# Loading order at the start of a fused SSM and SwiGLU kernel: tile 3 moved to ScalarE's queue behind a wait, up weights moved forward

## The chip, the cores and the metric

One core of one Trainium2 chip. The metric is device time in microseconds (us).

## The reference, cut to what matters

A layer norm over 2048 tokens of 448 features feeds a state-space model `s` and a gated feed-forward network; the output is `x + s * silu(ffn)`.

```python
xn = _layernorm(x, axis=-1)                      # x: 2048 x 448, bf16
s = _A_ref(xn, ...)                              # complex diagonal scan, D = P = 448
g = _silu((_silu(xn @ w_gate) * (xn @ w_up)) @ w_down)   # 448 -> 1792 -> 448
return x + s * g
```

The tokens are cut into 16 tiles of 128 rows. The first quarter is tiles 0 to 3. The 448 features are three blocks of 128 and a fourth block of the last 128, which overlaps the third.

## The kernel before: the parts that matter

The start loads tile 0 and the first weights on SyncE, tiles 1 and 2 on ScalarE:

```python
warm(11, D)                                     # filler matmuls until tile 0 is there
load_x1(0)                                      # SyncE
load_x(1, 3, nc.scalar)                         # ScalarE: tiles 1 and 2
nc.scalar.activation(of_table[:], half_pi[:], ACT.Sqrt)    # brings the table in
load_w(Wg, B_w_gate, 0, 512)                    # 384 KB (3 blocks), then 128 KB (last block)
load_x1(3)
load_w(Wu, B_w_up, 0, 512, part=0)              # 384 KB
for h in (H2, H1):                              # last block in two halves of 64 rows
    nc.sync.dma_start(out=Wu[h, KF, 0:512], in_=B_w_up[blk(KF), 0:512][h])
load_gu(512, 1024)                              # and so on: more weights, tiles 4 to 7, ...
```

The layer norm of tiles 0 to 3, in the order of the program (VectorE works in order; tile 2's sums are done by ScalarE):

```python
ln_stats(0); ln_std(0); act_part(2, 0)          # VectorE, ScalarE, ScalarE
ln_stats(1, ...); ln_std(1)
...                                             # tiles 0 and 1: norm, transposes, copies
act_part(2, 1)                                  # ScalarE: squares of tile 2
nc.scalar.activation(std[:, 2:3], ..., ACT.Sqrt, ...)
ln_stats(3)                                     # VectorE: statistics of tile 3
ln_std(3)
for n in range(2, TQ):                          # TQ = 4
    ln_inverse(n)                               # VectorE
    ln_norm(n)                                  # VectorE: xn[2], then xn[3]
```

On TensorE the first blocks run as a left half (tiles 0 and 1: gate, then up) and a right half (tiles 2 and 3). The transposes of tiles 2 and 3 sit among the up matmuls of the left half, in program order. Each transfer is also tied to a slot: from the ninth on, a SyncE load waits until an earlier one with its slot has landed.

## Time and profile before

| | before |
|---|---|
| median of the first 3 runs | 181.67 us (181.45 to 182.03) |
| span of the profile | 180.0 us |
| TensorE busy | 175.6 us, 98% |
| tile 0 lands | 3.1 us |
| tile 3 issued, lands | 2.17, 6.37 us |
| first matmul of the right half | 9.47 us |

The span is counted from the first instruction. A landing is the start of the issue plus the profile's time from issue to landing. The lines behind this table stand in the prediction. From the right half on TensorE has no gap, so that moment fixes the end.

### The profile page before, as it was taken

The numbers are of one execution on the slowest core, as the hardware profiler recorded it, in microseconds if no ns is written. First come the engines' busy times: TensorE is split into PE (matmuls) and PEld (weight loads), VectorE is DVE, ScalarE is ACT, GpSimd is POOL, SyncE is SP. The second block draws the span as 40 slices with busy tenths as digits, with TensorE's granted clock in tenths as the row PEclk, the third lists the DMA queues.
The fourth block names the chain that finished last, engine by engine and source line by source line (L and its number), as shares of the span: only waits on it lengthen the run. The fifth ranks groups of instructions, "written<-read, shape, count | busy, mean of one in ns | idle before, by whom it ended". The sixth has DMA issues, their size and how long they took to land.

```text
span 180.0 us, 3870 instructions
## 1 busy us (share of the span) xinstructions
PE 175.6 (98%) x1505; PEld 91.4 (51%) x1505; DVE 164.8 (92%) x271; ACT 122.1 (68%) x258; POOL 14.8 (8%) x24
## 2 busy tenths in 40 slices
PE   8999999999999999999999999999999999999992
PEld 3685555555555555555454444444444555555551
DVE  4869799999999989989999999999999999998872
ACT  4858779997779999299589997789676223101110
POOL 7022400000000000701400000000000000000001
PEclk9999999999999999999999999999999999999998
DMA  6996466889000000044000250000000001001111
GB/s 182 321 361 181 101 131 78 167 240 374 13 0 4 2 0 4 0 85 136 2 4 0 47 69 5 0 4 0 0 4 0 0 26 55 27 0 51 51 55 51
DMA packets 25074, 12.72 MB, mean 71 GB/s; under 512 B 14944, under 2 KB 25056, under 8 KB 25056
## 3 DMA queue, kind: packets, MB, share of 16 engines
q1 hardware_dynamic: 24512, 12.18, 26.1%
q10 hardware_dynamic: 416, 0.30, 0.5%
q8 instruction: 12, 0.20, 0.4%
q14 instruction: 6, 0.05, 0.1%
q0 software_dynamic: 128, 0.00, 0.0%
HBM read 7.23 MB, written 1.84 MB: 50 GB/s over the span
## 4 chain that ended last, share of the span: by engine, by line
PE 95%; DVE 2%; DMA 1%; issue 0%
PE gp L482 25%; PE hd L631 24%; PE up L482 20%; PE y L669 12%; PE pb L482 12%; PE one L482 2%; DMA x_all<-in_A_x_dram 1%; DVE stats_of L269 1%; DVE xn L283 0%; DVE ob L695 0%; DVE t L691 0%; DVE mv L272 0%; PE tp L335 0%; DVE rstd L708 0%; PE y L675 0%
## 5 line engine op out<-in xcount | busy, mean ns | idle before, releaser
L482 PE MATMUL gp<-xT,Wg 64*128 64x512 bf16 (+2 forms) x400 | 82.4, 364 | 0.0
L482 PE MATMUL up<-xT,Wu 64*128 64x512 bf16 (+2 forms) x400 | 82.2, 364 | 0.0
L482 PEld LDWEIGHTS <-Wg 64*128 64x128 bf16 x444 | 38.4, 94 | 22.5
L482 PEld LDWEIGHTS <-Wu 64*128 64x128 bf16 x428 | 38.2, 94 | 17.7 <-DMA Wu<-in_B_w_up_dram 0.2
L631 PE MATMUL hd<-Wd,Vt 128*128 128x448 bf16 x224 | 43.5, 352 | 0.0
L618 ACT ACTIVATE gs<-gp 128x512 bf16<-128x512 f32 x52 | 32.1, 617 | 10.7 <-PE gp L482 10.7
L619 ACT ACTIVATE us<-up 128x512 bf16<-128x512 f32 x52 | 32.4, 623 | 0.0
L631 PEld LDWEIGHTS <-Vt 128*128 128x128 bf16 x224 | 21.8, 98 | 20.5 <-DVE H_im L556 0.2
L636 ACT ACTIVATE sg<-hd 128x448 bf16<-128x448 f32 x16 | 8.4, 536 | 29.7 <-PE hd L631 29.6
L482 PE MATMUL pb<-xT,BT 64*128 64x512 bf16 (+1 forms) x224 | 21.9, 349 | 0.0
L623 DVE TENSOR_TENSOR Vt<-gs,us 128x2048 bf16<-128x2048 bf16 (+1 forms) x16 | 17.2, 1073 | 0.1
L482 PEld LDWEIGHTS <-BT 64*128 64x128 bf16 x224 | 11.7, 94 | 10.4 <-issue 0.4
L562 DVE TENSOR_TENSOR_SCAN bu_re<-rcol,H_re,ere 128x512 bf16<-128x512 f32 x12 | 15.2, 1270 | 0.1
L517 ACT ACTIVATE bu_re<-pb 128x512 bf16<-128x512 f32 (+1 forms) x20 | 10.0, 530 | 4.2 <-PE pb L482 4.1
L562 DVE TENSOR_TENSOR_SCAN bu_im<-rcol,H_im,eim 128x512 bf16<-128x512 f32 x9 | 11.4, 1262 | 0.0
L669 PE MATMUL y<-C,H_re 128*128 128x448 bf16 x48 | 11.0, 353 | 0.0
L319 ACT ACTIVATE xn<-x_all,off_of,rstd 128x384 bf16<-128x384 bf16 (+1 forms) x16 | 8.3, 622 | 3.4 <-POOL off_of L313 3.4
L691 DVE TENSOR_TENSOR t<-t,sg 128x448 f32<-128x448 f32 x15 | 9.4, 625 | 1.1
L527 ACT ACTIVATE bu_im<-bu_re 64x512 bf16<-64x512 bf16 x16 | 10.0, 628 | 0.3
L695 DVE TENSOR_TENSOR sg<-t,x_all 128x448 bf16<-128x448 f32 x15 | 9.4, 625 | 0.5
L556 DVE TENSOR_TENSOR tmp<-bu_im,ST 128x2048 bf16<-128x2048 bf16 x8 | 9.7, 1216 | 0.0
L669 PE MATMUL y<-C,H_im 128*128 128x448 bf16 x36 | 8.8, 352 | 0.0
(126 smaller groups left out, 191.0 us busy)
## 6 DMA issues: line engine op xcount, KB each, us to landing
out_dram<-sg SPq DMA_DIRECT2D x15, 112.0 KB, 1.7
Wd<-in_B_w_down_dram SPq DMA_DIRECT2D x1, 1568.0 KB, 10.1
Wg<-in_B_w_gate_dram SPq DMA_DIRECT2D x3, 384.0 KB, 4.9
Wu<-in_B_w_up_dram SPq DMA_DIRECT2D x3, 384.0 KB, 5.3
x_all<-in_A_x_dram SPq DMA_DIRECT2D x1, 896.0 KB, 5.2
x_all<-in_A_x_dram SPq DMA_DIRECT2D x2, 224.0 KB, 5.9
Wg<-in_B_w_gate_dram SPq DMA_DIRECT2D x3, 128.0 KB, 4.7
Wu<-in_B_w_up_dram SPq DMA_DIRECT2D x2, 128.0 KB, 5.3
```

Of the source, the lines that this page charges most:

```text
L482: mm = nc.tensor.matmul(out[:, a:b], lhsT=w[h, d, :], rhs=xT[h, d, q * W + c0 + a : q * W + c0 + b], start=(first and m == 0 and cut is cu ...
L517: nc.scalar.activation(to, pair[i][0], ACT.Copy)
L527: nc.scalar.activation(out[a], in_[b], ACT.Copy)
L556: nc.vector.tensor_tensor(out=of(out, n), in0=of(a, n), in1=of(b, n), op=op)
L562: nc.vector.tensor_tensor_scan(out=T["b"][c][:, k, :], data0=rcol[:, k : k + 1].to_broadcast([P, W]), data1=T["e"][c][:, k, :], initial=in ...
L618: nc.scalar.activation(gs[:, i + j, :], gp_[:], ACT.Silu)
L619: nc.scalar.activation(us[:, i + j, :], up_[:], ACT.Copy)
L623: nc.vector.tensor_tensor(out=Vt[:, f0 : f0 + n, :], in0=gs[:, 0:n, :], in1=us[:, 0:n, :], op=ALU.mult)
L631: nc.tensor.matmul(hd, lhsT=Vt_of[q][:, fi, j * P : (j + 1) * P], rhs=Wd[:, fi, :], start=(fi == 0), stop=(fi == NF - 1),)
L669: nc.tensor.matmul(y[:, c0:c1], lhsT=h, rhs=C2[:, n, c0:c1], start=(n == 0), stop=(n == NS - 1))
L691: nc.vector.tensor_tensor(out=t[:], in0=y, in1=sg[:, c0:c1], op=ALU.mult)
L695: adds.tensor_tensor(out=ob, in0=t[:], in1=x_all[:, m, c0:c1], op=ALU.add)
```

## The change

Its evident intent: free SyncE of one issue, so that the up weights come third on its queue; keep tile 3 from disturbing tile 0 by the wait; load the last up rows to all 128 partitions at once; split the large down load.

```diff
-    load_x1(0)
+    first = load_x(0, 1)
     load_x(1, 3, nc.scalar)
     of_table = ctile([P, 1], F32, "of_table")
     nc.scalar.activation(of_table[:], half_pi[:], ACT.Sqrt)
+    behind(nc.scalar, first)
+    load_x(3, 4, nc.scalar)
     load_w(Wg, B_w_gate, 0, 512)
-    load_x1(3)
-    load_w(Wu, B_w_up, 0, 512, part=0)
-    for h in (H2, H1):
-        nc.sync.dma_start(out=Wu[h, KF, 0:512], in_=B_w_up[blk(KF), 0:512][h])
+    load_w(Wu, B_w_up, 0, 512)
     load_gu(512, 1024)
...
-        nc.sync.dma_start(out=Wd[:], in_=B_w_down.rearrange("(ft p) d -> p ft d", p=P))
+        for half in (slice(0, NF // 2), slice(NF // 2, NF)):
+            nc.sync.dma_start(
+                out=Wd[:, half, :], in_=B_w_down.rearrange("(ft p) d -> p ft d", p=P)[:, half, :]
+            )
```

(The helper `load_x1` goes, and `load_x` returns its instruction. `behind` is an empty instruction that waits for a transfer.)

More of the change, by code (lines that the diff above doesn't have):

```diff
@@ L134 @@
     SYNC = mybir.DependencyInfo(mybir.DependencyClass.Sync, mybir.DependencyReason.DATA)
-    def load_x1(n):
-        nc.sync.dma_start(out=x_all[:, n, :], in_=x2d[n * P : (n + 1) * P, :])
     def load_x(n0, n1, eng=nc.sync):
-        eng.dma_start(
+        return eng.dma_start(
             out=x_all[:, n0:n1, :],
```

## The prediction

> **What bounds the kernel now.** I read the page first (busy shares and the forty slices), then the chain of waits, then the busy time by stretch, then the timeline of the first ten microseconds with each early transfer's time to landing. The page says where to look:
>
> ```profile
> span 180.0 us, 3870 instructions
> PE 175.6 (98%) x1505; PEld 91.4 (51%) x1505; DVE 164.8 (92%) x271; ACT 122.1 (68%) x258; POOL 14.8 (8%) x24
> PE   8999999999999999999999999999999999999992
> DMA  6996466889000000044000250000000001001111
> PE 95%; DVE 2%; DMA 1%; issue 0%
> ```
>
> TensorE is busy 98% of the span, and 95% of the chain that ended last is its matmuls. The transfers are dense only in the first ten slices and short bursts later. So a change to loads can act in one way only: by moving the moment at which TensorE is fully fed. The busy times by stretch (columns: stretch, length, PE, PEld, DVE, ACT, POOL, granted clock, DMA share, GB/s) say where that moment is:
>
> ```profile
> 0.00:5.90 5.90, 4.93 (x44) 2.14 (x45) 3.35 (x23) 2.80 (x7) 3.73 (x14) 1.00 0.73 222
> 5.90:10.00 4.10, 4.10 (x112) 3.65 (x110) 3.02 (x12) 3.66 (x10) 0.00 (x0) 1.00 1.01 322
> 10.00:177.00 167.00, 166.60 (x1360) 85.61 (x1354) 158.00 (x236) 115.60 (x242) 10.84 (x10) 1.00 0.24 60
> 177.00:180.00 3.00, 0.00 (x0) 0.00 (x0) 0.40 (x1) 0.00 (x0) 0.22 (x1) 0.82 0.13 38
> ```
>
> From 10 us to the end of the matmuls TensorE is busy 166.60 of 167.00; the missing 0.40 is its own end at 176.6. A load that lands earlier there gains nothing. Before 5.9 us TensorE runs filler matmuls and waits for tile 0 through the layer norm. What the change can touch is between 5.9 and 10 us, where the columns say busy but the ends of matmuls are modelled, so I look at the instructions:
>
> ```profile
> 0.72 2.37 DMA x_all<-in_A_x_dram
> 3.12 0.64 DVE stats_of L269
> 5.91 1.83 PE L482 MATMUL one<-xT,Wg 64*128 64x128 bf16 x44
> 6.35 0.63 DVE L269 BATCH_NORM_STATS2 stats_of<-x_all 128x6 f32<-128x448 bf16 x1
> 7.54 0.24 PEld L482 LDWEIGHTS <-Wu 64*128 64x128 bf16 x5
> 7.96 0.33 PEld L482 LDWEIGHTS <-Wu 64*128 64x128 bf16 x7 [0.18 <-DMA Wu<-in_B_w_up_dram]
> 8.20 0.31 PEld L335 LDWEIGHTS <-xn 64*128 64x128 bf16 x6
> 9.47 0.22 PE L482 MATMUL gp<-xT,Wg 64*128 64x128 bf16 x1
> ```
>
> The reader is to see three things. Tile 0 lands at 3.1 us and starts everything. The only wait of TensorE for a weight in the whole run is 0.18 us at 7.96, for the last up rows. The tile-3 statistics start at 6.35, just when tile 3 lands.
>
> The early landings, from issue start plus the time to landing of each issue (in us): tile 0 0.72+2.4=3.1; tiles 1 and 2 (ScalarE) 0.73+2.9=3.6; gate 384 KB 1.18+4.0=5.2; gate 128 KB 1.65+4.2=5.85; tile 3 2.17+4.2=6.35; up 384 KB 2.64+4.9=7.55; the two up halves of 64 rows 3.12+4.8=7.9 and 3.72+4.4=8.1.
>
> **What the Trainium skill says.** (1) "DMA: Bandwidth & Descriptors", section "Queues, rings and completion order": SyncE and ScalarE each own a ring on each of the same 16 DMA engines, and an engine takes turns between rings, packet by packet. The trace agrees: the 224 KB of tiles 1 and 2 landed at 3.6 on ScalarE's ring while 384 KB of gate, issued 0.45 us later on SyncE's, took until 5.2. (2) Same page, "Issuing engines are not separate DMA queues": a second issuing engine only saves sequencer time. An issue on SyncE is seen to take 0.4 to 0.6 us. (3) "SBUF — State Buffer", section "Door 1: The DMA port swizzle": a transfer to partitions 0 to 63 reaches only half of the ports. The trace fits: between 6.25 and 7.25 us, when the two 64-row halves should pass, the engines moved 212 GB/s, against 361 in the microsecond before and 351 in the one after. (4) "TensorE: Matmul & The Clock Gate", section "Wait — 56ns, not 53.3ns?": matmuls follow each other at columns over 2.4 GHz plus 2.5 ns when warm. The trace agrees: the 512-column matmuls of one array half start at 32.99, 33.20, 33.42, 33.63 us, 0.21 to 0.22 apart.
>
> **The change part by part.**
>
> Tile 3 to ScalarE behind tile 0. Removed from SyncE: one issue of 0.43 us and 112 KB ahead of the up weights. Added on ScalarE: a wait for tile 0 (about 3.1 us) and an issue of about 0.46 us (as its first one took), so 3.15 to 3.6. ScalarE is idle from 2.7 to 4.01 in the timeline, waiting for tile 0's mean: free. First data comes about 1 us after an issue (the engines start moving about 1.75 us, the first issue is at 0.72), so tile 3 shares the engines from about 4.15 and, by analogy with tiles 1 and 2, lands 2.4 to 2.9 us after issue: 5.6 to 6.1 instead of 6.35. VectorE reaches its statistics only after the copies that end at 6.28. Gain at most 0.07 us; and the next thing, the inverse deviation of tile 2 at 7.34, waits for ScalarE's square root that ends at 7.30, not for tile 3. So tile 3 earlier is worth nothing on TensorE's path.
>
> Up weights third, last 128 rows in one load. The issues move from 2.64, 3.12, 3.72 to about 2.17 and 2.65. But the stream is limited by rate: 0.98 MB lie ahead of the up weights in both kernels, since tile 3 only changes ring. The 384 KB should land at 7.2 to 7.55. Its last rows follow at the full rate: 128 KB at 360 GB/s is 0.36 us, against about 0.7 us for two half-rate loads. So all of the up weights are in by about 7.6 to 7.9 instead of 8.1, while what TensorE first asks for, the upper half, came at 7.9 before. Most of the 0.18 us wait may go. Ceiling: TensorE's work between 5.91 and 9.47 is 16 steps of 0.056 and 6 of 0.109 on gate (1.54), 14 of 0.109 on up (1.53), two tiles' transposes at about 0.13 each and the parameters' 0.06: 3.39 of 3.56 us. So no order of loads can win more than about 0.17 us there. And part is not free: the transposes of tile 2 started at 8.20 after a normalisation that ended at 8.02, so TensorE can come forward about 0.1 us before it waits for that instead. My estimate: 0.1 us.
>
> Ring slots. The order listing shows that each SyncE transfer, from the ninth in the program, waits for the one eight earlier. There is one transfer fewer up front, so the next gate load goes at about 3.1 rather than 4.36; the last 128 up rows of the second group now wait for tile 3 (about 6.0) and go about when they went before (6.00). Later loads come some 0.4 us earlier (the half-rate loss). Nobody on the path wants them: the second weight group landed at 9.3 to 11.1 and is used from about 12.4; tiles 4 and 5 (VectorE waited 1.22 us for them until 12.62) come earlier, which helps VectorE, not TensorE. Worth 0.
>
> Down weights in two loads. One more issue of about 0.57 us on SyncE at about 37 us; the load landed at 36.6+10.1=46.7 and its first reader starts at 59.5. Even 1 us later costs 0.
>
> Sum: 0.1 us gained, 181.67 to about 181.57.
>
> **The rivals.** (a) The new transfer on ScalarE's ring takes turns with the gate weights, which were ahead of it in one ring before. Gate's last 128 KB landed at 5.85 and is first needed at about 6.08 (the fourth matmul pair after 5.91): slack 0.2 us. Tile 3's 0.115 MB at 360 GB/s could push it back by up to 0.32 us: a new wait of 0.1 us on gate, which would eat the gain: 181.7. For it: the same round robin that made tiles 1 and 2 fast. Against it: at 4.15 only some 0.19 MB of gate is left. (b) Tile 3 lands late (after 6.28) because it is issued 1 us later. VectorE is in order, so its statistics would hold back tile 2's normalisation too, with some 0.1 us of slack: 0.5 us late would be 0.4 us on the end: 182.0. Against it: its ring is empty. (c) The freed ring slots and the full-rate load give more than I count, all of the 0.17 us and an earlier normalisation: 181.4. (d) Everything is hidden and only the scatter shows: 181.67 give or take 0.3.
>
> **Range and chances.** The scatter of the kernel before is 181.45 to 182.03. Around 181.55, with the rivals from 181.4 to 182.0 and a median's scatter of about 0.2, I take 181.1 to 182.1. A gain of 2% is 3.6 us, twenty times the ceiling of 0.17; a loss of 2% would need a stall that no margin above is near to. Faster 0.01, within 2% 0.98, slower 0.01.
>
> **What would show it.** Right: up weights' wait near 7.96 gone or under 0.1 us; the matmuls that start at 9.47 start at 9.3 to 9.45; the rate does not dip at 6.25 to 7.25; TensorE busy from there to 176.5; the down loads land before 50. Wrong: a wait of TensorE for gate weights near 6.1 (rival a); tile-3 statistics starting after 6.5 (rival b); any wait of TensorE for a weight or a tile after 12 us; an end of the matmuls that moves by more than 0.3 us.

## The result, and the profile after

The changed kernel takes 183.06 us in the median of 6 runs (182.59 to 183.66), against 181.7 (181.45 to 182.03) for the kernel before in the same rounds: ratio 1.0076, 95% interval 1.0056 to 1.0096. That is within 2%, as forecast, but 1.4 us slower and outside the range 181.1 to 182.1.

The page of the changed kernel: span, busy times, TensorE in forty slices.

```profile
span 181.3 us, 3871 instructions
PE 175.5 (97%) x1505; PEld 91.5 (50%) x1505; DVE 164.7 (91%) x271; ACT 122.1 (67%) x258; POOL 14.6 (8%) x24
PE   8789999999999999999999999999999999999992
```

No engine has more work than before (TensorE 175.5 against 175.6). The 1.3 us by which the span grew are idle time, and the slices place it in the second and third (7 and 8 where it was 9 and 9). The busy times by stretch (the columns are those of the prediction: stretch, length, PE, PEld, DVE, ACT, POOL, clock, DMA share, GB/s):

```profile
0.00:5.90 5.90, 4.61 (x44) 2.18 (x44) 3.36 (x23) 2.80 (x7) 3.74 (x14) 1.00 0.70 207
5.90:10.00 4.10, 2.99 (x79) 2.44 (x72) 1.99 (x8) 2.30 (x6) 0.00 (x0) 1.00 1.09 355
...
10.70:177.80 167.10, 167.10 (x1375) 86.19 (x1370) 158.00 (x237) 116.26 (x245) 10.22 (x9) 1.00 0.23 58
```

From 5.9 to 10 us TensorE is busy 2.99 us where it was busy all 4.10. From the first matmul of the right half on it is busy 167.10 of 167.10 us; the same piece of work in the kernel before:

```profile
9.47:176.50 167.03, 167.03 (x1375) 86.14 (x1370) 157.83 (x237) 116.13 (x244) 10.39 (x9) 1.00 0.24 61
```

The same 1375 matmuls in the same time: everything behind the right half's start is merely moved. The question is what held that start back. The chain of waits of the changed kernel, its first 11 us (start, length, what):

```profile
0.73 2.44 DMA x_all<-in_A_x_dram
...
3.24 4.85 DMA x_all<-in_A_x_dram
...
8.11 0.64 DVE stats_of L265
...
9.12 0.41 DVE xn L279
```

Before, the chain ran through tile 0, TensorE's first matmuls and nothing more of DMA. Now it runs through tile 0, then straight into a second transfer of 4.85 us, tile 3, and from there over VectorE. The instructions in the timeline:

```profile
3.24 0.36 ACTq L138 DMA_DIRECT2D x_all<-in_A_x_dram  x1
...
7.54 0.64 PEld L478 LDWEIGHTS <-Wu 64*128 64x128 bf16 x12
...
8.11 0.63 DVE L265 BATCH_NORM_STATS2 stats_of<-x_all 128x6 f32<-128x448 bf16 x1 [1.76 <-DMA x_all<-in_A_x_dram]
...
9.57 0.17 PEld L331 LDWEIGHTS <-xn 64*128 64x128 bf16 x8 [1.39 <-DVE xn L279]
...
10.70 0.22 PE L478 MATMUL up<-xT,Wu 64*128 64x128 bf16 x1
```

Read it beside the lines of before in the prediction, and beside this one, tile 2's normalisation before:

```profile
7.62 0.40 DVE L283 TENSOR_SCALAR xn<-x_all,mv,rstd 128x448 bf16<-128x448 bf16 x1
```

The up weights load without a wait at 7.54: the wait of 0.18 us is gone. But tile 3's statistics start at 8.11 instead of 6.35, so tile 2 is normalised at 9.12 instead of 7.62, TensorE's transposes of tile 2 start at 9.57 instead of 8.20, the right half at 10.70 instead of 9.47, and the last matmul group at 177.51 instead of 176.19. Tile 3 landed at 3.24 + 4.8 = 8.04 us, 1.67 later than before.

### The profile page after: what moved, and what is told of

Same layout as the page of the kernel before. It is cut to its first block, busy times and chain, and to the rows that moved or that the text cites. A ratio compares the mean times of both kernels' runs of the same rounds, so it can differ in the third digit from the quotient of the medians.

```text
span 181.3 us, 3871 instructions
## 1 busy us (share of the span) xinstructions
PE 175.5 (97%) x1505; PEld 91.5 (50%) x1505; DVE 164.7 (91%) x271; ACT 122.1 (67%) x258; POOL 14.6 (8%) x24
## 4 chain that ended last, share of the span: by engine, by line
PE 93%; DMA 4%; DVE 1%; issue 0%; DVEq 0%; ACTq 0%
PE gp L478 25%; PE hd L627 23%; PE up L478 20%; PE y L665 12%; PE pb L478 12%; DMA x_all<-in_A_x_dram 4%; PE one L478 0%; DVE stats_of L265 0%; DVE xn L279 0%; DVE ob L691 0%; DVE t L687 0%; PE gp L331 0%; DVE mv L268 0%; PE y L671 0%; PE up L331 0%
```

## The experiments

The theory to test: tile 3's late landing is the whole loss, and it lands late because a transfer is served behind all that were issued before it, on either queue. The wait delays its issue until SyncE has the up weights issued ahead of it. Rivals: the up or down loads or the shifted slots cost; ScalarE's queue, or its wait, is slow in itself; VectorE's order is the greater part.

| kernel | tile 3's queue | issued | KB issued ahead | landed | right half starts | median us | ratio (95%) |
|---|---|---|---|---|---|---|---|
| before | SyncE | 2.17 | 848 | 6.4 | 9.47 | 181.7 | 1 |
| changed | ScalarE, wait | 3.24 | 1744 | 8.0 | 10.70 | 183.06 | 1.0076 (1.0056 to 1.0096) |
| t3_sync | SyncE | 2.17 | 848 | 6.3 | 9.41 | 181.63 | 0.9992 (0.9978 to 1.0005) |
| t3_alone | ScalarE, wait | 2.88 | 1296 | 8.3 | 10.91 | 182.83 | 1.0061 (1.0045 to 1.0078) |
| t3_sync_late | SyncE | 3.18 | 1360 | 7.9 | 10.51 | 182.93 | 1.0061 (1.0045 to 1.0078) |
| up_gated | ScalarE, wait | 3.08 | 848 | 5.9 | 10.37 | 182.17 | 1.002 (0.9995 to 1.0044) |
| t3_at_once | ScalarE | 1.2 | 720 | 6.2 | 9.67 | 181.91 | 1.0001 (0.9982 to 1.002) |
| t3_no_wait | ScalarE | 1.29 | 720 | 5.5 | 10.23 | 182.28 | 1.0027 (1.0001 to 1.0054) |
| t3_mid | SyncE | 2.65 | 1232 | 7.75 | 10.31 | 182.66 | 1.0033 (1.0012 to 1.0054) |
| dve_order | ScalarE, wait | 2.99 | 1360 | 8.4 | 10.71 | 183.09 | 1.0067 (1.0049 to 1.0085) |
| up_one_load | SyncE | 2.17 | 848 | 5.8 | 9.48 | 181.76 | 0.9995 (0.998 to 1.0009) |

The KB are those of the loads (tiles and weights) whose issue began earlier; the 1744 of the changed kernel include 384 KB of gate issued only 0.06 us before. "Right half" is the start of its first matmul in the profile. The 181.7 us of before are from the rounds of the changed kernel; in the rounds of the other rows before had medians of 181.82, 181.82 and 181.69, and each ratio is taken to those of its own rounds. The landings are of one profile each. They fall into two groups, 5.5 to 6.4 us with 720 to 848 KB ahead and 7.75 to 8.4 with 1232 to 1744; within a group the KB do not order them.

**t3_sync: tile 3 back, the rest of the change kept.**

```diff
-    behind(nc.scalar, first)
-    load_x(3, 4, nc.scalar)
     load_w(Wg, B_w_gate, 0, 512)
+    load_x(3, 4)
     load_w(Wu, B_w_up, 0, 512)
```

> The changed kernel with tile 3 put back on SyncE between the gate and the up weights, no wait on ScalarE; up rows in one load and down weights in two stay. Theory (the tile's late landing is the whole loss, because a transfer is served behind all that were issued before it on either queue): tile 3 lands at 6.2 to 6.4 us, its statistics start near 6.3, no wait for a weight near 8 us, 181.4 to 181.8 us. Rival (the loss comes from the up or down loads or from the shifted ring slots): stays near 183.

As the theory said: statistics at 6.26, 181.63 us. So the up load in one piece and the down load in two cost nothing that these runs can see, and tile 3's move holds the whole loss. This was the fastest version that was run, but its interval includes 1: it does not clearly beat the kernel before.

**t3_alone: on the kernel before, only tile 3 moves.**

```diff
+    behind(nc.scalar, first)
+    load_x(3, 4, nc.scalar)
     load_w(Wg, B_w_gate, 0, 512)
-    load_x1(3)
```

(Cut here: `first = load_x(0, 1)` for `load_x1(0)`, and the helper's return.)

> The kernel before with only tile 3 moved to ScalarE behind tile 0; the up rows stay in two halves, the down weights in one load. Theory: some 1.3 MB are issued ahead of it, so it lands at 7.6 to 8.1 us and the time is 182.7 to 183.3. Rival (the loss needs the up weights ahead in one load, or is from elsewhere): below 182.2.

The time is inside the expected band, the landing 0.2 us behind it. The part alone brings 0.61%, an interval that overlaps the whole change's. Its timeline shows the same wait (and two shorter ones, of 0.24 and 0.47 us, of the weight loads for up rows):

```profile
8.33 0.63 DVE L270 BATCH_NORM_STATS2 stats_of<-x_all 128x6 f32<-128x448 bf16 x1 [2.34 <-DMA x_all<-in_A_x_dram]
...
9.79 0.17 PEld L336 LDWEIGHTS <-xn 64*128 64x128 bf16 x8 [1.32 <-DVE xn L284]
```

**t3_sync_late: the same moment of issue on the other queue, no wait.**

```diff
-    behind(nc.scalar, first)
-    load_x(3, 4, nc.scalar)
     load_w(Wg, B_w_gate, 0, 512)
     load_w(Wu, B_w_up, 0, 512)
+    load_x(3, 4)
```

> The changed kernel with tile 3 on SyncE behind the up weights, without any wait, so it is issued at about 3.2 us as in the changed kernel but on the other queue. Theory (order of issue decides, not the queue): it lands at 7.6 to 8.0, 182.6 to 183.1 us. Rival (ScalarE's queue or the wait is what is slow): it lands before 7 and the time is under 182.2.

```profile
3.18 0.43 SPq L138 DMA_DIRECT2D x_all<-in_A_x_dram  x1
...
7.92 0.63 DVE L264 BATCH_NORM_STATS2 stats_of<-x_all 128x6 f32<-128x448 bf16 x1 [1.89 <-DMA x_all<-in_A_x_dram]
```

Issued 0.06 us earlier on SyncE, it landed at 7.9 against 8.0. The packets say the same: the first of tile 3's started at 5.94 us here, in SyncE's queue behind the up rows, and at 5.91 in the changed kernel, where it was alone on ScalarE's. Neither ScalarE's queue nor the wait instruction is slow in itself; nor does a queue of its own help. That agrees with the Trainium skill, "DMA: Bandwidth & Descriptors", section "Issuing engines are not separate DMA queues": the second queue saved issue time alone (SyncE's next gate load went at 3.65 us here and at 3.18 in the changed kernel).

**up_gated: same queue, same wait, nearly the same moment (3.08 for 3.24 us), but fewer loads ahead.** The first up load on SyncE, and so all behind it, waits for tiles 1 and 2.

```diff
-    load_x(1, 3, nc.scalar)
+    second = load_x(1, 3, nc.scalar)
...
+    behind(nc.sync, second)
     load_w(Wu, B_w_up, 0, 512)
```

> The changed kernel with the first up load and all SyncE loads after it held until tiles 1 and 2 have landed (about 3.6 us), so tile 3, issued on ScalarE behind tile 0 at about 3.24 as in the changed kernel, has only the gate weights ahead. Theory (order of issue): it lands at 5.8 to 6.5, statistics near 6.3 to 6.5, up weights by about 8, 181.5 to 182.1 us. Rival 1 (ScalarE's ring loses its turns while SyncE has work queued): it lands at 7.5 or later, near 183. Rival 2 (the wait on ScalarE itself costs): near 183 too.

Tile 3 landed at 5.9 us, 2.8 us after its issue instead of 4.8. This is the sharpest pair with the changed kernel. What each queue moved between 3.6 and 5.5 us (queue: packets, MB, share of the 16 engines; q1 is SyncE's, q10 ScalarE's), first in the changed kernel:

```profile
q1 hardware_dynamic: 608, 0.59, 98.8%
```

and in up_gated:

```profile
q1 hardware_dynamic: 405, 0.38, 73.2%
q10 hardware_dynamic: 144, 0.11, 17.8%
```

In the changed kernel not one packet of tile 3 moves in these 1.9 us, although it was issued at 3.24. In up_gated, with only the gate weights ahead, all of it moves, the first packet 1.2 us after the issue. Later, from 5.5 to 8 us, the changed kernel's two queues:

```profile
q1 hardware_dynamic: 742, 0.72, 85.4%
q10 hardware_dynamic: 144, 0.11, 18.9%
```

Its 144 packets come in this stretch, mixed with the last up rows and the next gate load.

One rival is not settled by this pair: that ScalarE's queue loses its turns whenever SyncE has work. While tile 3 moved in up_gated, from 4.5 to 5.0 us, SyncE's queue was nearly empty (32 packets, against tile 3's 128), because the held up weights came only afterwards. The next run answers it.

The time of up_gated missed the expectation slightly (182.17 for 181.5 to 182.1), for another reason: the up weights, held back, landed at 3.67 + 4.8 = 8.5 us, and TensorE waited for them (the idle time in the line is that of the weight loads; the matmuls themselves were idle for 0.78 us).

```profile
8.54 0.66 PEld L479 LDWEIGHTS <-Wu 64*128 64x128 bf16 x12 [1.06 <-DMA Wu<-in_B_w_up_dram]
```

**t3_at_once: without the wait, right behind tiles 1 and 2.**

```diff
     load_x(1, 3, nc.scalar)
+    load_x(3, 4, nc.scalar)
...
-    behind(nc.scalar, first)
-    load_x(3, 4, nc.scalar)
```

> The changed kernel with tile 3 issued on ScalarE right behind tiles 1 and 2 (about 1.2 us), no wait: only tiles 0 to 2 and the first gate load are ahead of it. Theory (order of issue): it lands at 4.0 to 5.0 us, the gate's last rows some 0.3 us later than before (5.6 to 6.0); the statistics of tile 3 then start when VectorE is free, near 6.25; 181.4 to 181.8 us, no better than before by more than 0.2, since tile 2's chain through ScalarE and not tile 3 sets the pace. Rival (ScalarE's ring is slow beside SyncE's): it lands after 6.5, over 182.2.

Landing and time were both missed: the landing by more than 1 us (6.2 for 4.0 to 5.0), the time by 0.1 (181.91 for 181.4 to 181.8, level with before in its rounds). The tile still came soon enough for VectorE, whose statistics started at 6.21. What the queues moved from 3.6 to 4.5 us:

```profile
q1 hardware_dynamic: 228, 0.22, 72.3%
q10 hardware_dynamic: 119, 0.10, 31.2%
```

Here SyncE's queue had the gate weights to move, issued from 1.18 us on, and tile 3, issued on ScalarE 0.05 us after the first of them, moved along with them. So ScalarE's queue does not lose its turns because SyncE has work; and the order of issue is not a strict one between loads issued almost together. 135 of the tile's 144 packets had started by 4.54 us. The other nine came one by one from 5.26 to 5.85, and they set the landing; why they were late stays open. The price appeared where rival (a) of the prediction had put it, on the last gate rows, landed at 1.65 + 4.7 = 6.35:

```profile
6.42 1.37 PEld L477 LDWEIGHTS <-Wg 64*128 64x128 bf16 x38 [0.50 <-DMA Wg<-in_B_w_gate_dram]
```

**t3_no_wait: only the wait goes, the place in the program stays.**

```diff
-    behind(nc.scalar, first)
     load_x(3, 4, nc.scalar)
```

> The changed kernel without the wait for tile 0, same place in ScalarE's program (behind the table load): issued at about 2.7 us, when nearly all of the first up weights are already issued. Theory: about 1.2 to 1.35 MB ahead, it lands at 7.2 to 7.8, the end follows the landing one for one beyond 6.35 or so: 182.2 to 182.9 us. Rival (the wait is what costs): as fast as before, 181.5 to 181.9.

A miss, although the time (182.28) fell into the expected band: that was luck, since neither the issue nor the landing was as said. I had put the issue at 2.7 us, behind the table load and the activation that stand ahead of it in ScalarE's program. It went at 1.29, beside the table load:

```profile
1.22 1.28 ACT L195 ACT_TABLE_LOAD   x1 [1.22 <-PEq L921]
1.29 0.43 ACTq L138 DMA_DIRECT2D x_all<-in_A_x_dram  x1
2.52 0.20 ACT L195 ACTIVATE of_table<-half_pi 128x1 f32<-128x1 f32 x1
```

So the wait puts the issue off by 3.24 - 1.29 = 1.95 us, and in that time SyncE issues the rest of gate, the up weights and the next gate load. Without it tile 3 landed at 5.5, but again at the gate's expense, by more than in t3_at_once:

```profile
6.97 1.37 PEld L477 LDWEIGHTS <-Wg 64*128 64x128 bf16 x38 [1.06 <-DMA Wg<-in_B_w_gate_dram]
```

The two kernels issue tile 3 within 0.1 us of each other, and their gate landings (6.35 and 6.95) differ by 0.6 us in one profile each. I draw nothing from that difference.

**t3_mid: a middle dose.**

```diff
-    load_w(Wu, B_w_up, 0, 512)
+    load_w(Wu, B_w_up, 0, 512, part=0)
+    load_x(3, 4)
+    load_w(Wu, B_w_up, 0, 512, part=1)
```

(and no tile 3 on ScalarE.)

> The changed kernel with tile 3 on SyncE between the two up loads (gate and 384 KB of up ahead of it, 1.2 MB in all). Theory (order of issue, and the end follows the landing once it is later than VectorE needs it at about 6.3): lands at 7.3 to 7.6, between the 6.3 of the tile ahead of the up weights and the 7.9 of the tile behind them; the end between theirs, 182.2 to 182.8 us. Rival (two states only, held or not held by something else): as 181.6 or as 182.9.

```profile
7.73 0.63 DVE L265 BATCH_NORM_STATS2 stats_of<-x_all 128x6 f32<-128x448 bf16 x1 [1.50 <-DMA x_all<-in_A_x_dram]
```

Landing 7.75, a little behind the expected 7.3 to 7.6; the median of 182.66 and the ratio of 1.0033 lie between those of t3_sync and t3_sync_late. But as a middle dose it is weak: the landing is only 0.15 us before that of t3_sync_late, the two intervals overlap (1.0012 to 1.0054, 1.0045 to 1.0078), and its weight loads also waited 0.25 us for gate. The rival of two states is not excluded by it. Along t3_sync, t3_mid, t3_sync_late tile 3 landed at 6.3, 7.75, 7.9 and the right half began at 9.41, 10.31, 10.51.

**dve_order: tile 2 ahead of tile 3's statistics on VectorE.**

```diff
+    ln_inverse(2)
+    ln_norm(2)
     ln_stats(3)
     ln_std(3)
     nc.scalar.activation(of_table[:], half_pi[:], ACT.Silu)
-    for n in range(2, TQ):
-        ln_inverse(n)
-        ln_norm(n)
+    ln_inverse(3)
+    ln_norm(3)
```

> The changed kernel with tile 2's normalisation ahead of tile 3's statistics on VectorE, so a late tile 3 does not hold tile 2 back. If VectorE's order were the larger part of the loss: below 182.2. My theory: tile 2's transposes return to about 8.2 us, but tile 3's own chain (statistics at 8.1, normalised by about 9.9) still holds TensorE until about 9.85 instead of 10.15: 182.6 to 183.0 us, 0.2 to 0.4 under the changed kernel.

Tile 2 was indeed set free, but the median of 183.09 is that of the changed kernel, so the gain that I expected is not seen. In its profile tile 2 is normalised early, and TensorE waits for tile 3 instead:

```profile
7.44 0.40 DVE L279 TENSOR_SCALAR xn<-x_all,mv,rstd 128x448 bf16<-128x448 bf16 x1
...
8.37 0.63 DVE L265 BATCH_NORM_STATS2 stats_of<-x_all 128x6 f32<-128x448 bf16 x1 [0.53 <-DMA x_all<-in_A_x_dram]
...
10.14 0.17 PEld L331 LDWEIGHTS <-xn 64*128 64x128 bf16 x8 [0.71 <-DVE xn L279]
```

In this profile tile 3 landed at 8.4, 0.35 later than in the changed kernel's, which could hide 0.2 us. What the runs do show is that VectorE's order is not the larger part of the loss: the tile itself is.

**up_one_load: the kernel before with one load for the last up rows.**

```diff
-    load_w(Wu, B_w_up, 0, 512, part=0)
-    for h in (H2, H1):
-        nc.sync.dma_start(out=Wu[h, KF, 0:512], in_=B_w_up[blk(KF), 0:512][h])
+    load_w(Wu, B_w_up, 0, 512)
```

> The kernel before with only the last 128 up rows in one load. Theory: no dip of the rate between 6.25 and 7.25 us, the wait of 0.18 us for up weights gone or shorter, 181.5 to 181.8 us, within 0.15 us of before. Rival (half-rate loads cost more than the wait shows): under 181.4.

The stretch from 6.25 to 7.25 us, in the kernel before (last column GB/s):

```profile
6.25:7.25 1.00, 1.00 (x33) 0.89 (x28) 0.85 (x3) 0.97 (x5) 0.00 (x0) 1.00 0.73 212
```

and in up_one_load:

```profile
6.25:7.25 1.00, 1.00 (x34) 0.88 (x30) 0.90 (x3) 0.97 (x4) 0.00 (x0) 1.00 0.99 290
```

The dip is mostly gone, and so is TensorE's wait for up weights; the right half began at 9.48 all the same, and the time did not move (0.9995). The dip agrees with the Trainium skill, "SBUF — State Buffer", section "Door 1: The DMA port swizzle", that the prediction named, by which partitions 0 to 63 reach only half of the ports: 212 GB/s while the 64-row halves pass, 290 with one load of 128 rows.

## Why the prediction was wrong, step by step

- *What bounds the kernel*: right. TensorE from the right half's first matmul on takes 167.0 to 167.1 us in both kernels, and only the start can move. No run contradicts the ceiling of 0.17 us on any gain: none was faster with an interval clear of 1. The runs are too coarse to confirm it (the interval of t3_sync reaches down to 0.9978, 0.4 us).
- *Tile 3 to ScalarE*: this is the step that failed. It said "by analogy with tiles 1 and 2, lands 2.4 to 2.9 us after issue: 5.6 to 6.1". Measured: 4.8 us after issue, 8.04. The moment of issue was right (3.15 said, 3.24 seen). The analogy was false: tiles 1 and 2 had been issued with 112 KB ahead of them, tile 3 behind more than 1.3 MB. Their quick landing had been read as taking turns between two rings, but fits the order of issue as well. Had turns been enough, tile 3 alone on its ring would have landed before the tile 3 of t3_sync_late, which stood behind the up rows on SyncE's; it did not (8.0 and 7.9). Turns at the start of a load were seen only in t3_at_once and t3_no_wait, with loads issued 0.05 and 0.11 us apart.
- *Rival (b)*: it was the one that came true, and its mechanism was right: VectorE's statistics of tile 3 held tile 2 and then TensorE, and its sign, statistics after 6.5, was seen (8.11). It was dismissed with "Against it: its ring is empty", and an empty ring gave no precedence. Its size followed the wrong landing: 0.5 us late was taken to cost 0.4; at 1.67 late the right half came 1.23 late and the last matmul group 1.32, so the slack was some 0.35 to 0.45, not 0.1.
- *Up weights*: the wait of 0.18 us went, as said, and the rate no longer dips (297 GB/s from 6.25 to 7.25 us for 212). They landed at 7.3 and 7.65 us, as said, although the 0.98 MB said to lie ahead of them counted tile 3, which in fact moved after most of them. The 0.1 us hoped for is not seen: t3_sync and up_one_load are within their scatter of before.
- *Ring slots*: the next gate load went at 3.18, as said. Wrong in a detail: I had the second group's last up rows waiting for tile 3; they went at 4.90, and it was the third group's gate load that went at 8.11, just after tile 3 landed (7.94 before). It cost nothing on the path.
- *Down weights in two*: right. They landed no later than 36.4 + 9.7 = 46.1 us, and t3_sync, which has them, is as fast as before.
- *Rival (a)*, a wait for gate weights: not in the changed kernel's profile, but it is what meets the versions that load tile 3 early (0.50 us and 1.06 us on the weight loads, 0.33 and 0.88 on the matmuls), and 0.53 us in dve_order's, whose first loads are those of the changed kernel, and 0.25 in t3_mid's. Over the profiles the last gate rows landed between 5.25 and 6.95 us, around the 6.08 at which the prediction saw them needed.
- *Range*: it followed from the sum and gave rival (b) only 0.4 us at the most, so it ended at 182.1.

What stays open: which part of the chip keeps the order between the two queues. The traces show when the packets move, not where they wait.

## What to carry to other kernels

When the transfer engines are saturated, ask of each load not which queue it is on but how many bytes were issued before it; a wait ahead of an issue gives up a place in that order, and an idle queue does not buy it back. The order is a coarse one: loads issued almost together on two queues moved together in t3_at_once. Before trusting an analogy between two transfers, compare what was ahead of each. A tile that must pass a long chain (statistics, normalisation, transposes) before its use deserves an earlier place than weights that are read directly, but only as far as the weights in front can spare.

## What the Trainium skill lacked or had wrong

- "DMA: Bandwidth & Descriptors", section "Queues, rings and completion order", says that each engine takes turns between rings, packet by packet. t3_at_once agrees, for loads issued 0.05 us apart: 119 packets on ScalarE's ring and 228 on SyncE's in the same 0.9 us. In the changed kernel tile 3 got no such turn: the 112 KB on ScalarE's ring, issued at 3.24 us, moved no packet until 5.91, while SyncE's ring moved 608 from 3.6 to 5.5 us (gate and up rows, issued by 2.65 us). The section does not say that loads issued earlier on another ring can go first.
- No page gives the landing of one load under backlog: here 112 KB took 2.4 us from issue with nothing ahead, 2.8 to 5.0 with 720 to 848 KB ahead, and 4.7 to 5.4 with 1.2 to 1.7 MB.
- "DMA: Bandwidth & Descriptors", section "Latency and other measured facts", gives about 600 ns to the first byte for SyncE and ScalarE and does not say from where it counts. In the kernel before the first issue starts at 0.72 us and takes 0.40, and the engines first move data at 1.75: about 1.0 us from the start of the issue, about 0.6 from its end.
